# A list scheduler for the last step of the first MoE, and a unit's first group between the products of the unit before it

## The chip, the cores and the metric

The kernel runs on one core of a Trainium2 chip. Its engines are TensorE (PE, matrix products; PEld its weight loads), VectorE (DVE), ScalarE (ACT), GpSimd (POOL) and SyncE (SP, which here issues all the DMAs). Each executes its own instructions strictly in program order and waits on semaphores for the others. The metric is the device time of one execution in microseconds (us). The trace is of one execution, and times in it count from the span's start.

## The reference

Delta-rule attention over 4 batches, 8 heads, 768 positions gives 3072 tokens of 384 numbers. They go through a dense leaky feed-forward layer (the first MoE) and then through eight experts (the second MoE):

```python
h = x @ w_in                                  # 384 -> 2048
x2 = np.maximum(0.01 * h, h) @ w_out          # 2048 -> 384
P = exp(x2 @ w_gate - max)                    # 3072 x 8
for _ in range(8):                            # row and column sums in turn
    P /= P.sum(1, keepdims=True) + 1e-09
    P /= P.sum(0, keepdims=True) + 1e-09
    P *= N / E
out = sum(P[:, e:e+1] * (np.maximum(x2 @ w1[e], 0) @ w2[e]) for e in range(8))   # 384 -> 1024 -> 384
```

All in fp32; the kernel splits each operand into a high and a low part and multiplies three times (high by high, low by high, high by low).

## The kernel before

**Steps and chunks.** The tokens are cut into six steps of 512 (`TB`: 128 positions of each of 4 batches). In a step the first MoE (`main_a`, L647) runs over 16 chunks of 128 hidden units. A chunk's first product is nine matmuls 128x512 into a `ph` bank (L632); ACT scales it by 0.01 (`leak`, L669), DVE takes the maximum (L670), ACT rounds it to the high part `gh` (L672), DVE or POOL subtracts for the low part `gl` (L674); the second product is nine matmuls into three `po` banks (L684). PE computes chunk i's first product, then chunk i-1's second one.

**Step 5**, the last one, is special: no attention is left, and beside it the second MoE is prepared as a background (`pre_c`). Between two pieces of `main_a` it emits a little of it: the scales from the maxima (`powers`, L572 to L592); for five steps of tokens the load of x2 (`load_x`) into a staging tile `stg` (there are four), its parts `gxh` (ACT, L837) and `gxl` (DVE, L838) and six matmuls for the gate (L700); for four chunk pairs of the first expert's weights the load, a scaling (ACT, L841), four sums each for w1 and w2 (POOL, L868 and L887), the high parts (ACT, L873 and L892) and low parts (POOL, L874 and L893); and the operands `xoh`, `xol` of two token steps (L849 to L854). `Stage` keeps the loads ahead. Every engine's order is the order in which the program writes this down.

**The second MoE** is 24 units: 8 experts e by 3 pairs p of token steps. Its products are by Strassen and Winograd: seven products of sub-blocks in place of eight, with sums of operands and results around them. A unit has four `Group`s (first products: 33 matmuls 128x512 each, L1040, in f16, with some fifteen DVE and ACT operations that make the seven hidden operands h0..h6 with high and low parts), and four `Pair`s of seven second products (12 matmuls 128x192 each, L1133). After a product DVE adds the bank to the output sums with the gate's weight (`put`, written at the helper L1018, for the first expert L1015 or a copy at L1164). In the first expert's units the Sinkhorn rounds run beside the products.

All of that is written as operations of a `Plan` (L57): each has an engine, a modelled duration, what it reads and writes, and a due time; the plan starts on each engine the ready operation with the earliest due time, and emits all of them in the order of the planned starts. PE's due times follow the order in which its operations are written. The helpers make all instructions from a few lines: L1012 is every ACT copy, L1015 every two-operand subtraction or sum, L1018 every fused one, on DVE unless POOL is named.

**Banks and ends of units.** There are eight PSUM banks: `b0` to `b5` and two named `ph` (6 and 7). Pair i keeps products 1, 6, 7 in bank x, products 4, 5, 3 in bank 6 whatever the pair, product 2 in bank 2:

```python
self.x, self.y, self.z = (0, 1, 5, 7 if e else 0)[i], 6, 2
```

After eleven products of mixed pairs, a pair's last four come together (6, 5, 7, 3), pair after pair. Product n of a pair takes the hidden operand that `PRODUCTS` names: product 6 takes h4, 5 takes h3, 7 takes h5 and 3 takes h6. A bank that was started anew has to be read by its `put` before PE may start it again. Behind the last product the program writes a `clear` matmul (L1322) and then the next unit's four groups; the planner draws two products of them, into b5, in front of the old unit's last two.

Of the kernel before, what the change touches and what calls it, by code (L numbers as in the profile page):

```python
# [57 lines left out]
class Plan:  # L58
# [27 lines left out]
    def run(self):  # L86
# [17 lines left out]
        while len(done) < len(self.ops):  # L104
# [28 lines left out]
def delta_moe_kernel(ctx: ExitStack, tc: tile.TileContext, k_l, v_l, q_l, beta_l, wa_in, wg, wc, out):  # L133
# [8 lines left out]
    def fr(ap):  # L142
        return ap.bitcast(F32)
# [507 lines left out]
    def main_a(t):  # L651
# [5 lines left out]
        for i in range(n + 1):  # L657
            k = first + i
            if i < n:
# [14 lines left out]
                (dve if t in (0, 1, NT - 1) else pool).tensor_tensor(out=gl, in0=g, in1=fr(gh), op=ALU.subtract)  # L674
# [12 lines left out]
        for c in range(KD):  # L687
            o = g_p.tile([128, TB], F32, tag="gl" if c == 2 else "leak", name="x2o")
            act.activation(out=o, in_=po[c], func=ACTF.Copy)
            dve.tensor_reduce(out=xmax[:, t, c:c + 1], in_=po[c] if t == NT - 1 else o, axis=AX.X, op=ALU.max,  # L690
# [4 lines left out]

    def gate_block(xh, xl, t, ps_fn, lt, ordered=lambda ins: None):
        ps = ps_fn()
        for i, x in enumerate((xh, xl)):
            for c in range(KD):
                ordered(pe.matmul(out=ps[0:32], lhsT=wg_r[:, c], rhs=x[c] if isinstance(x, list) else x[:, c],  # L700
                                  start=(i == 0 and c == 0), stop=(i == 1 and c == KD - 1)))
            yield
        ordered(dve.transpose(out=lt.rearrange("p g e -> p (g e)"), in_=ps[0:32]))
        ordered(dve.tensor_tensor(out=logits[:, t * TB // 32:(t + 1) * TB // 32], in0=lt[:, :, 0:E],
                                  in1=lt[:, :, E:2 * E], op=ALU.add))
        yield

    if True:
# [119 lines left out]
        def staging():  # L828
            return cst_p.tile([128, KD * TB], F32, tag="stg", name="stg")

        def load_x(t):
            s = staging().rearrange("p (c n) -> p c n", c=KD)
            sp.dma_start(out=s, in_=x2_dram[t].rearrange("c p n -> p c n"))
            return s

        def parts(hi, lo, src, lo_eng):
            act.activation(out=hi, in_=src, func=ACTF.Copy)  # L837
            lo_eng.tensor_tensor(out=lo, in0=src, in1=fr(hi), op=ALU.subtract)  # L838

        def scaled(x, col):  # L840
            ordered(act.activation(out=x, in_=x, func=ACTF.Copy, scale=scl[:, col:col + 1]))  # L841

        def make_xo(s, t, tt):
            i, flat = t % 2, s.rearrange("p c (n k) -> p (c n) k", n=2)
            scaled(s, 2 * E + t)
            yield
            for o, x, y in ((tt[:, 0], flat[:, 1], flat[:, 0]), (tt[:, 1], flat[:, 3], tt[:, 0]),
                            (tt[:, 2], flat[:, 3], flat[:, 1]), (tt[:, 3], flat[:, 2], tt[:, 1])):
                pool.tensor_tensor(out=o, in0=x, in1=y, op=ALU.subtract)  # L849
            yield  # L850
            for j, src in ((slice(0, 1), flat[:, 0:1]), (slice(1, 5), flat[:, 2:6]), (slice(5, 9), tt)):
                hi, lo = (x[:, j, i] for x in xo)
                ordered(act.activation(out=hi, in_=src, func=ACTF.Copy))
                pool.tensor_tensor(out=lo, in0=src, in1=hi, op=ALU.subtract)  # L854
                yield

        def load_w1(n):
            e, k = divmod(n, NF2 // 2)
            s = staging()[:, 0:1280].rearrange("p (j f) -> p j f", f=128)
# [34 lines left out]

        def none(arg, s):
            pass

        W1, W2 = (load_w1, sums_w1, make_w1), (load_w2, sums_w2, make_w2)

        class Stage:  # L900
# [529 lines left out]
```

## Time and profile before

| | |
|---|---|
| median of three runs | 2382.3 us (2381.95 to 2382.96) |
| the profiled execution, its span | 2374.54 us, 2372.8 us |
| attention with steps 0 to 4 of the first MoE | 0 to 844 us |
| step 5 with the preparation | 844 to 947 us |
| second MoE, first expert | 947 to 1139 us |
| second MoE, experts 1 to 7 | 1139 to 2369 us |

A window row gives the stretch, its length, then the busy time, with the number of instructions, of PE, PEld, DVE, ACT and POOL in this order, then PE's granted clock (1.00 is 2.4 GHz, 0.50 is 1.2 GHz), the DMA engines' busy share and GB/s. Length less PE's busy time is PE's idle time. A timeline row gives start, duration, engine, line, output and inputs; in brackets stands how long the engine was idle just before, and what ended that.

### The profile page before, as it was taken

What the parts mean: (1) busy time and instruction counts of PE and PEld (TensorE: products, weight loads), DVE (VectorE), ACT (ScalarE), POOL (GpSimd) and SP (SyncE); (2) the same over time, 40 slices, a digit from 0 to 9 for tenths busy, and PEclk for the clock granted to TensorE, in tenths of its full rate; (3) what the DMA queues carried; (4) which work ended last, traced back from release to release, by engine and by line L of the source; (5) the groups of instructions that cost most, each with busy time, mean ns of one, the idle gap of its engine ahead of it and who ended that gap; (6) DMA issues with size and microseconds to landing.
All of it is one profiled execution on the core that took longest, in us unless ns stands there. A gap on an engine that the chain in (4) does not pass through costs nothing.

```text
span 2372.8 us, 43674 instructions
## 1 busy us (share of the span) xinstructions
PE 2200.5 (93%) x17324; PEld 1664.1 (70%) x17324; DVE 1702.5 (72%) x3304; ACT 1432.9 (60%) x2632; POOL 680.9 (29%) x748
## 2 busy tenths in 40 slices
PE   6788799999999988989999999999999999999999
PEld 5676677777777766666667677677677677677676
DVE  8567876848574254888677777777777777777777
ACT  6878757465655554666766655655655655656554
POOL 5444402132332254222411421321311312312100
PEclk7678999989999999999999999999999999999999
DMA  3354575545544353323323323323323333323221
GB/s 115 123 187 157 188 264 166 182 157 165 200 150 145 122 211 127 106 76 140 121 101 121 114 101 121 114 101 121 114 100 122 117 109 123 109 103 131 98 102 51
DMA packets 123453, 312.90 MB, mean 132 GB/s; under 512 B 14960, under 2 KB 66800, under 8 KB 117104
## 3 DMA queue, kind: packets, MB, share of 16 engines
q1 hardware_dynamic: 123248, 310.11, 38.2%
q8 instruction: 136, 2.23, 0.4%
q14 instruction: 69, 0.57, 0.1%
HBM read 247.84 MB, written 62.13 MB: 131 GB/s over the span
## 4 chain that ended last, share of the span: by engine, by line
PE 57%; DVE 8%; ACT 2%; POOL 2%; issue 1%; DMA 0%; SPq 0%; DVEq 0%; ACTq 0%; POOLq 0%
PE b L1040 18%; PE ph L1133 13%; PE ph L1040 10%; PE b L1133 10%; PE po L684 1%; PE ph L632 1%; DVE acc L1018 1%; DVE h26l L1015 1%; DVE h36l L1015 1%; DVE c L1018 1%; DVE h35l L1015 1%; DVE h16l L1015 1%; POOL stg L887 0%; DVE gxl L838 0%; POOL w1l L874 0%
## 5 line engine op out<-in xcount | busy, mean ns | idle before, releaser
L1015 POOL TENSOR_TENSOR stg<-stg 128x128 f32<-128x128 f32 (+2 forms) x240 | 157.4, 676 | 900.0 <-ACT stg L1012 896.0
L1040 PEld LDWEIGHTS <-w1h 128*128 128x128 f16 x2112 | 206.2, 98 | 241.6 <-issue 7.9
L1040 PE MATMUL b<-xoh,w1h 128*128 128x512 f16 x672 | 254.7, 379 | 0.0
L1040 PE MATMUL b<-xoh,w1l 128*128 128x512 f16 x672 | 254.7, 379 | 0.0
L1040 PE MATMUL b<-xol,w1h 128*128 128x512 f16 x672 | 254.7, 379 | 0.0
L684 PE MATMUL po<-gh,w 128*128 128x512 f32 (+1 forms) x600 | 221.2, 412 | 11.6 <-ACT gh L672 11.4
L1018 DVE SCALAR_TENSOR_TENSOR acc<-ph,pm,acc 128x192 f32<-128x192 f32 x315 | 134.8, 428 | 134.2 <-PE ph L1133 132.6
L1012 ACT ACTIVATE b<-ph 128x512 f32<-128x512 f32 x288 | 165.9, 584 | 72.6 <-PE ph L1040 66.7
L1040 PEld LDWEIGHTS <-w1l 128*128 128x128 f16 x1056 | 103.4, 98 | 124.6
L632 PE MATMUL ph<-x1h,w 128*128 128x512 f32 (+1 forms) x600 | 184.4, 414 | 4.9 <-DMA w<-wa_scratch 2.9
L1018 DVE SCALAR_TENSOR_TENSOR c<-b,v 128x512 f32<-128x512 f32 x96 | 66.1, 688 | 137.5 <-PE b L1040 131.6
L1012 ACT ACTIVATE v<-b 128x512 f32<-128x512 f32 x96 | 57.1, 595 | 173.6 <-PE b L1040 172.3
L670 DVE TENSOR_TENSOR leak<-leak,ph 128x512 f32<-128x512 f32 (+1 forms) x100 | 66.0, 660 | 117.6 <-ACT leak L669 115.0
L1040 PE MATMUL ph<-xoh,w1h 128*128 128x512 f16 x384 | 145.5, 379 | 4.2 <-ACT b L1012 4.2
L1040 PE MATMUL ph<-xoh,w1l 128*128 128x512 f16 x384 | 145.5, 379 | 0.0
L1040 PE MATMUL ph<-xol,w1h 128*128 128x512 f16 x384 | 145.5, 379 | 0.0
L684 PEld LDWEIGHTS po<-gh,w 128*128 128x128 f32 x600 | 117.3, 198 | 36.9 <-ACT gh L672 16.6
L1012 ACT ACTIVATE c<-b 128x512 f32<-128x512 f32 x192 | 114.3, 595 | 40.7 <-PE b L1040 39.9
L1015 DVE TENSOR_TENSOR c<-c,c 128x512 f32<-128x512 f32 x192 | 134.2, 705 | 1.4
L1018 DVE SCALAR_TENSOR_TENSOR c<-c,c 128x512 f32<-128x512 f32 x192 | 131.6, 698 | 2.0
L684 PE MATMUL po<-gl,w 128*128 128x512 f32 (+1 forms) x300 | 123.9, 414 | 9.5 <-POOL gl L674 6.0
L632 PEld LDWEIGHTS ph<-x1h,w 128*128 128x128 f32 x600 | 113.1, 201 | 27.3 <-DMA w<-wa_scratch 3.3
(433 smaller groups left out, 6924.1 us busy)
## 6 DMA issues: line engine op xcount, KB each, us to landing
w<-wa_scratch SPq DMA_DIRECT2D x100, 768.0 KB, 4.4
acc_scratch<-acc SPq DMA_DIRECT2D x84, 384.0 KB, 2.7
acc<-acc_scratch SPq DMA_DIRECT2D x84, 384.0 KB, 3.7
wraw<-wc SPq DMA_DIRECT2D x128, 192.0 KB, 3.3
stg<-wc SPq DMA_DIRECT2D x64, 384.0 KB, 8.7
xoh<-xo_scratch SPq DMA_DIRECT2D x21, 1152.0 KB, 5.1
xol<-xo_scratch SPq DMA_DIRECT2D x21, 1152.0 KB, 8.2
raw<-wa SPq DMA_DIRECT2D x48, 256.0 KB, 3.0
```

Source lines behind the costliest of these rows:

```text
L632: pe.matmul(out=ps, lhsT=wt[:, c * 128:(c + 1) * 128], rhs=xx[:, c], start=(n == 0), stop=(n == 3 * KD - 1))
L670: dve.tensor_tensor(out=g, in0=g, in1=ps, op=ALU.max)
L684: pe.matmul(out=po[c][:, cols], lhsT=wt[:, DM + c * 128:DM + (c + 1) * 128], rhs=xx, start=(i == 1 and m == 0), stop=(i == n and m == 2), ...
L1012: return vec("ACT", n, lambda e: e.activation(out=out, in_=src, func=func, scale=scale), reads, writes, **kw)
L1015: return vec(eng, n, lambda e: e.tensor_tensor(out=out, in0=a, in1=b, op=fn), reads, writes, **kw)
L1018: return vec("DVE", n, lambda e: e.scalar_tensor_tensor(out=out, in0=a, scalar=scalar, in1=b, op0=f0, op1=f1), reads, writes, **kw)
L1040: ordered(pe.matmul(out=banks[b], lhsT=w[:, a], rhs=x[:, c].rearrange("p s k -> p (s k)"), start=start, stop=i == 2 and (a, c) == terms[-1 ...
L1133: ordered(pe.matmul(out=banks[b][:, 0:HD], lhsT=xx[:, o:o + 128], rhs=wt[:, t], start=first and k == 0 and j == 0, stop=k == NK - 1 and j ...
```

## The change

Three edits:

1. In `Plan.run` a PE operation that follows another PE operation may be planned as soon as PE is free, not after the other's latency.
2. Step 5 of the first MoE and the preparation are written as operations of a plan of their own, with chunk i's second product behind two thirds of chunk i+1's first product as the written order. A gate's six matmuls become one piece. The sums of the first expert's weights go from POOL to DVE (`eng="DVE"`), and the parts of w2 are made in three pieces (192, 576, 576 columns) instead of two. The maxima at the step's end are taken from the copies, not from the `po` banks. `gate_block`, `Stage` and the loaders go.
3. In the second MoE banks are given out anew, the products of different pairs alternate to the end, and a group is cut into seven steps. The next unit's first group (`ahead`) runs its steps between the unit's last five products, except where the next unit's operands are still being made on the chip (two of the first expert's ends). The loads of the next operands are written behind the last group, not at the unit's end. For the first expert the copies after a product go from DVE to ACT.

```diff
@@ Plan.run
-                s.ready = max(s.ready, end + (self.WAIT if s.eng != e else 0.0))
+                s.ready = max(s.ready, end + self.WAIT if s.eng != e else free[e] if e == "PE" else end)
@@ step 5
-        bgq.add("pre_c", pre_c)
-        for _ in main_a(NT - 1):
-            bgq.spend(1.0, 2)
-        while bgq.pending():
-            bgq.pump(2)
+        tasks = {}
+        for n, t in enumerate((2, 3, 4, 0, 1)):
+            tasks[(2, 5, 8, 10, 12)[n]] = (n, t)
...
+        for i in range(NF1):
+            if i + 1 < NF1:
+                first_of(i + 1, (0,))
+            if i:
+                cks[i - 1].second()
+                if i + 3 < NF1:
+                    last = [cks[i + 3].load(last)]
+            if i in tasks:
+                n, t = tasks[i]
+                s, j = load_step(t)
+                gate(t, s, j, n)
+                if t < 2:
+                    operands(t, s, j)
+                else:
+                    weight1(t - 2, eng="DVE")
+                    weight2(t - 2, eng="DVE")
+            if i + 1 < NF1:
+                first_of(i + 1, (1, 2))
+        weight1(3, eng="DVE")
+        weight2(3, eng="DVE")
+        cks[NF1 - 1].second()
...
+        plan.run()
@@ Group: banks; head and body become seven steps with a yield behind each
-                self.x, self.y, self.z, self.w, self.v = 7 - k % 2 if e else 6, 2, 3, 4, 5
+                self.x, self.y, self.z, self.w, self.v = k % 2 * 7, 1, 3, 4, 5 if k else 3
@@ Pair: banks
-                self.x, self.y, self.z = (0, 1, 5, 7 if e else 0)[i], 6, 2
+                self.x, self.y, self.z = (0, 1, 5, 7)[i], 6 if e else 3 + i % 2, 2
+                self.y5 = (6, 2, 6, 2)[i] if e else (3, 4, 2, 2)[i]
@@ Pair.put
                 if self.e == 0 and fresh:
-                    vec("DVE", n, lambda e: e.tensor_copy(out=o, in_=src), [("ps", b)], [("acc", blk)])
+                    copy(n, o, src, [("ps", b)], [("acc", blk)])
@@ order of the products
-            for i, q in [(i, q) for i in range(4 if e else 3) for q in (6, 5, 7, 3)]:
+            for i, q in [(1, 1), (0, 2), (0, 4), (2, 1), (1, 2), (1, 4), (3, 1), (2, 2), (2, 4), (3, 2), (3, 4),
+                         (0, 6), (1, 6), (2, 6), (3, 6), (0, 5), (1, 5), (0, 7), (0, 3), (1, 7), (1, 3), (2, 5)]:
                 x[i].product(q)
                 if (i, q) == (0, 6):
                     mark = [x[0].last]
...
+            if nxt and not made:
+                ahead = Group(*nxt, 0)
+                it = ahead.steps()
+                clear(1, hb[0][S1][0][:, 0:128], hb[0][S1][0], [("h", 0, S1, 0)])
+                next(it)
+            for i, q in ((3, 5), (2, 7), (2, 3), (3, 7), (3, 3)) if e else ((2, 7), (2, 3), (3, 5), (3, 7), (3, 3)):
+                x[i].product(q)
+                if ahead:
+                    next(it)
...
+            for _ in it if ahead else ():
+                pass
```

**What moves on ACT in step 5.** These are ACT's rows before, near the end of the preparation (`w1h`, `w2h`: high parts of weights; `leak`, `gh`: a chunk of the first MoE; in brackets what a row waits for):

```order
L873 ACTIVATE w1h_9558<-stg 128x384
L669 ACTIVATE leak<-ph 128x512 [waits PE_49]
L873 ACTIVATE w1h_9558<-stg 128x768
L841 ACTIVATE stg<-stg,scl 128x768 [waits DMAHW2_49]
L672 ACTIVATE gh<-leak 128x512 [waits DVE_49]
L892 ACTIVATE w2h_9568<-stg 128x192 [waits Activation_49]
L892 ACTIVATE w2h_9568<-stg 128x1152 [waits Pool_49]
L669 ACTIVATE leak<-ph 128x512 [waits PE_49]
```

And these are the rows at the same place of the changed kernel, where L945 and L949 are the chunk's two operations and L835 is every copy of the preparation:

```order
L835 ACTIVATE stg<-stg,scl 128x768 [waits DMAHW0_49,Pool_49]
L835 ACTIVATE w2h_9566<-stg 128x576
L945 ACTIVATE leak<-ph 128x512 [waits PE_49]
L835 ACTIVATE w2h_9568<-stg 128x192 [waits Activation_49]
L949 ACTIVATE gh<-leak 128x512 [waits DVE_49]
L835 ACTIVATE w1h_9558<-stg 128x768 [waits DVE_49]
L835 ACTIVATE w2h_9568<-stg 128x576
L945 ACTIVATE leak<-ph 128x512 [waits PE_49]
L949 ACTIVATE gh<-leak 128x512 [waits DVE_49]
L835 ACTIVATE w2h_9568<-stg 128x576
```

Before, the copy 128x1152 that waits for POOL's sums stands ahead of a chunk's `leak`. After, no high part there waits for POOL (the scaling waits for its staging tile to be free), the large one is two pieces, and never more than two operations of the preparation stand between two of the chunks'.

**What moves on PE at the end of a unit.** PE's rows before (L1133 with h03h begins product 5 of a pair, with h05h product 7, with h06h product 3; L1322 is the clear; L1040 with b5 belongs to the next unit's first group, w1h0, and its second, w1h1; the rows left out are weight loads and the further matmuls of each product):

```order
L1133 MATMUL ph_10349<-w2h4_9570,h03h_10276 128x192 [waits DVE_49]
...
L1133 MATMUL ph_10350<-w2h4_9570,h05h_10280 128x192 [waits DVE_49]
...
L1133 MATMUL ph_10349<-w2h4_9570,h06h_10282 128x192 [waits DVE_49]
...
L1322 MATMUL b2_10345<-h00h_10270 128x512
...
L1040 MATMUL b5_10348<-xoh_9546,w1h0_9552 128x512 [waits DVE_49]
...
L1133 MATMUL ph_10349<-w2h4_9570,h03h_10276 128x192 [waits DVE_49]
...
L1040 MATMUL b5_10348<-xoh_9546,w1h1_9554 128x512 [waits Activation_49]
...
L1133 MATMUL ph_10349<-w2h4_9570,h06h_10282 128x192 [waits DVE_49]
...
L1040 MATMUL ph_10350<-xoh_9546,w1h0_9552 128x512 [waits DVE_49]
```

PE's rows of the changed kernel (L1182 is a second product, L1308 the clear, L1083 a first product; xoh with w1h0 belongs to the next unit):

```order
L1182 MATMUL ph_10342<-w2h2_9566,h03h_10269 128x192 [waits DVE_49]
...
L1308 MATMUL b1_10337<-h03h_10269 128x512 [waits DVE_49]
...
L1083 MATMUL b0_10336<-xoh_9546,w1h0_9552 128x512 [waits DMAHW3_49]
...
L1182 MATMUL b2_10338<-w2h2_9566,h03h_10269 128x192 [waits DVE_49]
...
L1083 MATMUL b3_10339<-xoh_9546,w1h0_9552 128x512
...
L1182 MATMUL b5_10341<-w2h2_9566,h05h_10273 128x192
...
L1083 MATMUL b0_10336<-xoh_9546,w1h0_9552 128x512 [waits Activation_49]
...
L1182 MATMUL ph_10342<-w2h2_9566,h06h_10275 128x192 [waits DVE_49]
...
L1083 MATMUL b1_10337<-xoh_9546,w1h0_9552 128x512
...
L1182 MATMUL ph_10343<-w2h2_9566,h05h_10273 128x192
...
L1083 MATMUL b0_10336<-xoh_9546,w1h0_9552 128x512 [waits Activation_49]
```

Before, the last products alternate between the two `ph` banks, most of them wait for DVE's `put` of an earlier one, and two first products stand among them. After, each of the last five products has a step of the next group's seven in front of it, and the five go to four banks.

## Rows read from the trace of the kernel before

**Rows 1.** Windows of three stretches: step 5, first expert, the other seven.

```profile
844.10:947.20 103.10, 84.11 (x322) 60.71 (x321) 54.10 (x76) 53.38 (x84) 60.73 (x62) 0.92 0.49 175
947.20:1138.60 191.40, 179.16 (x1438) 126.58 (x1438) 155.61 (x319) 116.27 (x192) 57.60 (x61) 0.99 0.31 110
1138.60:2369.40 1230.80, 1195.81 (x9851) 860.57 (x9848) 944.20 (x1680) 732.57 (x1294) 283.71 (x331) 0.99 0.31 109
```

**Rows 2.** Waits of PE in step 5: total us, times, longest.

```profile
PE po L684 <- ACT gh L672: 6.3, 4, 2.3
PE gate L700 <- ACT gxh L837: 4.0, 2, 3.0
PE po L684 <- DVE gl L674: 3.4, 3, 2.0
PE gate L700 <- DVE gxl L838: 2.6, 4, 1.3
```

**Rows 3.** Chain of waits, end of step 5: start, us, what.

```profile
930.75 2.04 PE ph L632 x9
...
945.28 1.90 DVE xmax L690 x3
```

**Rows 4.** Groups of step 5: busy us, mean ns; idle before and its releasers.

```profile
L887 POOL TENSOR_TENSOR stg<-stg 128x192 f32<-128x192 f32 x16 | 11.4, 733 | 0.2
...
L868 POOL TENSOR_TENSOR stg<-stg 128x128 f32<-128x128 f32 x16 | 10.3, 666 | 16.4 <-ACT stg L841 16.1
...
L838 DVE TENSOR_TENSOR gxl<-stg,gxh 128x512 fp32r<-128x512 f32 x15 | 16.1, 1106 | 5.6 <-ACT gxh L837 3.4 <-DMA stg<-wc 2.2
L674 DVE TENSOR_TENSOR gl<-leak,gh 128x512 fp32r<-128x512 f32 x16 | 15.3, 957 | 14.2 <-ACT gh L672 14.2
```

**Rows 5.** Timeline of DVE and POOL at 860 us.

```profile
860.85 2.45 DVE L674 TENSOR_TENSOR gl<-leak,gh 128x512 fp32r<-128x512 f32 x1 [3.79 <-ACT gh L672]
...
860.38 2.37 POOL L893 TENSOR_TENSOR w2l<-stg,w2h 128x1152 f16<-128x1152 f32 x1 [1.27 <-ACT w2h L892]
```

**Rows 6.** Windows within step 5.

```profile
844.10:850.00 5.90, 5.14 (x24) 3.67 (x23) 5.05 (x13) 3.76 (x8) 0.00 (x0) 1.00 1.00 355
860.00:870.00 10.00, 7.14 (x18) 4.48 (x19) 7.58 (x8) 7.42 (x14) 7.63 (x8) 0.66 0.44 159
```

**Rows 7.** Waits of PE, first expert.

```profile
PE ph L1133 <- DVE acc L1164: 6.7, 4, 2.4
PE ph L1040 <- ACT b L1012: 4.2, 6, 1.0
```

**Rows 8.** Waits of PE, experts 1 to 7.

```profile
PE ph L1133 <- DVE acc L1018: 17.6, 21, 1.0
PE b L1133 <- DVE acc L1018: 17.4, 8, 2.8
```

**Rows 9.** Windows of two units of expert 5, clear to clear.

```profile
1841.27:1901.46 60.19, 56.77 (x472) 40.77 (x470) 46.53 (x80) 38.17 (x67) 24.17 (x27) 1.00 0.33 117
1901.46:1958.96 57.50, 56.60 (x471) 40.76 (x470) 44.58 (x80) 31.30 (x56) 6.94 (x7) 1.00 0.27 99
```

**Rows 10.** Timeline of PE and DVE near those units' ends.

```profile
1890.42 0.24 PE L1133 MATMUL b<-w2h,h05h 128*128 128x192 f16 x1 [2.44 <-DVE acc L1018]
...
1892.55 0.24 PE L1133 MATMUL ph<-w2h,h06h 128*128 128x192 f16 x1 [0.98 <-DVE acc L1018]
...
1950.06 0.24 PE L1133 MATMUL ph<-w2h,h06h 128*128 128x192 f16 x1 [0.90 <-DVE acc L1018]
...
1889.36 0.68 DVE L1015 TENSOR_TENSOR h35l<-c,h35h 128x512 f16<-128x512 f32 x1
1889.96 0.41 DVE L1018 SCALAR_TENSOR_TENSOR acc<-b,pm,acc 128x192 f32<-128x192 f32 x1
```

**Rows 11.** Windows of 20 us, units of expert 3: groups, products.

```profile
1440.00:1460.00 20.00, 20.00 (x95) 9.10 (x93) 18.88 (x31) 17.73 (x34) 0.00 (x0) 1.00 0.06 21
1480.00:1500.00 20.00, 20.00 (x173) 14.79 (x172) 8.35 (x18) 11.06 (x20) 15.26 (x23) 1.00 0.53 170
```

More of the change, by code (lines that the diff above doesn't have):

```diff
@@ L843, in make_xo @@
[L843 to L855, printed above, removed]
@@ new lines, in gate, with emit @@
+        def gate(t, s, j, g):
+            for c in range(KD):
+                copy(TB, gx[0][:, c], s[:, c], [("stg", j)], [("gx", 0, c)])
+                tensor(TB, gx[1][:, c], s[:, c], fr(gx[0][:, c]), ALU.subtract, [("stg", j), ("gx", 0, c)],
+                       [("gx", 1, c)], shared=True)
+            b, P = gb[g % 2], ("bg", g % 2)
+            def emit():
+                for i in range(2):
+                    for c in range(KD):
+                        ordered(pe.matmul(out=b[0:32], lhsT=wg_r[:, c], rhs=gx[i][:, c], start=i == 0 and c == 0,
+                                          stop=i == 1 and c == KD - 1))
+            op("PE", 2 * KD * MR, 2 * KD * MR + 0.15, emit, [("gx", i, c) for i in range(2) for c in range(KD)], [P])
+            op("DVE", 0.7, 0.8, lambda: [ordered(dve.transpose(out=lt.rearrange("p g e -> p (g e)"), in_=b[0:32]))],
+               [P], ["lt"])
+            op("DVE", 0.3, 0.4, lambda: [ordered(dve.tensor_tensor(
+                out=logits[:, t * TB // 32:(t + 1) * TB // 32], in0=lt[:, :, 0:E], in1=lt[:, :, E:2 * E],
+                op=ALU.add))], ["lt"], [("logits", t)])
@@ new lines, in delta_moe_kernel @@
+        for i in range(2, 4):
+            last = [cks[i].load(last)]
+        gen = powers(0, NSC, lambda name: gb[2], ordered)
+        first_of(0, (0,))
+        for eng, us in (("PE", 0.4), ("DVE", 1.0), ("PE", 0.4), ("DVE", 1.4)):
+            op(eng, us, us + 0.1, lambda: next(gen), [("bg", 2)], [("bg", 2)])
+        first_of(0, (1, 2))
+        for i in range(NF1):
[16 more added lines that the diff above has]
+                first_of(i + 1, (1, 2))
@@ L1025, in delta_moe_kernel @@
+        rate = 170e3
         class Group:
@@ L1332, in delta_moe_kernel @@
                     dma(128 * 9 * TB * 2, xo_dram[p, i], xo[i].rearrange("p j s k -> p (j s k)"), XO, [("xod", p, i)])
-            gs = [Group(e, p, k) for k in range(NK)]
+            gs = [ahead] if ahead else [Group(e, p, 0)]
+            gs += [Group(e, p, k) for k in range(1, NK)]
             for k, g in enumerate(gs):
-                g.head()
+                if not ahead or k:
+                    it = g.steps()
+                    next(it)
                 if k:
                     gs[k - 1].tail()
-                g.body()
+                for _ in it:
+                    pass
             if e:
@@ L1341, in delta_moe_kernel @@
                 load(e, p, 2)
+            nxt = units[u + 1] if u + 1 < len(units) else None
+            made = e == 0 and p < 2
             x = [Pair(e, p, i) for i in range(4)]
@@ L1354, in delta_moe_kernel @@
                     mark = [x[0].last]
-            if not e:
-                for q in (1, 2, 4, 6, 5, 7, 3):
-                    x[3].product(q)
-            if u + 1 < len(units):
-                clear(2, hb[0][A11][0][:, 0:128], hb[0][A11][0], [("h", 0, A11, 0)])
-            n = (e + 1) * NK
-            if e == 0 and p < 2:
+            n = (e + 1) * NK
+            ahead = None
+            if e == 0:
+                for b in (3, 4):
+                    clear(b, hb[0][S1][0][:, 0:128], hb[0][S1][0], [("h", 0, S1, 0)])
+            if nxt and not made:
+                ahead = Group(*nxt, 0)
[5 more added lines that the diff above has]
+                if ahead:
+                    next(it)
+            if nxt and made:
+                clear(1, hb[0][S1][0][:, 0:128], hb[0][S1][0], [("h", 0, S1, 0)])
                 ss = [load_step(t) for t in (2 * p + 2, 2 * p + 3)]
```

384 lines of the change are left out of this document (171 added, 213 removed).

## Prediction

> **What bounds the kernel now.** First the table of windows: in all three stretches that the change touches PE is the busiest engine, but not to the same degree. Its idle time is the length less its busy time: step 5 has 103.10 - 84.11 = 19.0 us, the first expert 191.40 - 179.16 = 12.2 us, experts 1 to 7 1230.80 - 1195.81 = 35.0 us [rows 1]. Step 5 is also the one with a low clock, 0.92. Second, PE's waits, stretch by stretch, to see who ends the idle time: in step 5 four different lines of ACT and DVE [rows 2], in the second MoE almost only DVE's additions to the output [rows 7, 8]. Third, what those engines did then: the groups and timelines [rows 4, 5, 10]. So PE's own work is the floor, and the change is worth what it takes away of 66 us of idle time and of the time at half clock.
>
> **Step 5, the floor.** 16 chunks of 2 x 9 matmuls are 288, and 30 are for the gates. After the preparation has ended, a chunk's nine take 2.04 us without a gap [rows 3], so 0.227 each: 288 x 0.227 = 65.3 and 30 x 0.227 = 6.8, together 72.1 us. Around it stand the start and the end. At the end PE's first clear waits for three maxima that DVE reads from the very banks to be cleared, 1.90 us behind a first copy [rows 3]; the changed kernel takes the maxima from ACT's copies, so the bank is free after the copies; I put 1.2 us for the end, and 0.9 us for the scales' transpose, which stands early in the new order. A step 5 without any other wait is 72.1 + 2.1 = 74 us, 29 less than the 103.1 of now.
>
> **Step 5, the waits that stay.** They are 6.3 + 4.0 + 3.4 + 2.6 = 16.3 us [rows 2], and what the low clock adds behind them (0.66 on the mean from 860 to 870 us, of levels that are 1.00 and 0.50 [rows 6]). Their cause is the program order: ACT takes copies of weights that wait for POOL's sums while a chunk's `leak` or `gh` is queued behind, and a gate's matmuls stand on PE ahead of a chunk that is ready. POOL's sums are 11.4 + 10.3 = 21.7 us of its 60.7 [rows 1, 4]. The changed order puts one chunk operation after every two operations or so of the preparation, waits for all parts of a gate before its six matmuls, and moves the 21.7 us to DVE. DVE has 54.1 us of 103.1 busy now [rows 1]. Nearest to the new operations on DVE are POOL's own rows, 0.67 to 0.73 us each [rows 4], of 128 or 192 columns, and DVE's `gl` of 512 columns, at 0.96 on the mean with its delays [rows 4]. By the one the 32 sums would cost DVE 22 us; by their share of `gl`'s width (0.25 and 0.375), 16 x 0.24 + 16 x 0.36 = 10 us, which is my estimate, since the engine and the operation are the same. DVE is then at 64 of about 80 us, ACT at its 53, POOL at 60.7 - 21.7 = 39. That is tighter than now, on an engine whose order mixes sums that wait for a load with the `gl` that PE waits for. The bounds are a gain of 29 (no wait stays) and of 0 (all stay, as the wait for DVE replaces the one for POOL). I take 20, nearer to the floor, since the stretch after the preparation shows PE at full rate with these same chunk operations on ACT and DVE [rows 3], and the waits that go are those that POOL's sums set. Each of the queues has cover: the DMAs move 175 GB/s x 103 us = 18 MB in the step, which at the 355 GB/s of its first 6 us [rows 1, 6] is 51 us.
>
> DVE and POOL do hinder each other here: `gl` took 2.45 us at 860.85 where POOL's `w2l` ran from 860.38 for 2.37 us [rows 5]. The Trainium skill, SBUF — State Buffer, section Who interferes with whom, has the rule: DVE and GpSimd share one pair of SBUF ports under an exclusive lock. The trace agrees with the rule by the 2.45 us. By it POOL holds DVE for less of the time, 39 instead of 61 us, but DVE has 32 more instructions to be held; were every second sum held for 1 us, DVE would be at 80 of 80 us and the gain of step 5 near half of the one I take.
>
> **Experts 1 to 7.** Here I go from clear to clear. A regular unit takes 57.50 us with PE busy 56.60; the first unit of expert 5, 60.19 [rows 9]. With 14 regular units in 1230.80 us the other seven take (1230.80 - 14 x 57.50) / 7 = 60.8 each. If a unit were PE's 56.6 and nothing else, 14 x 0.9 + 7 x 4.2 = 42 us would go; 35.0 of that is idle time [rows 1], the rest is the clock. What sets the waits is the banks: product 3 of a pair waits until DVE has read the bank of product 5, 0.90 us at 1950.06 and 21 such waits in all, 17.6 us; in the longer units product 7 waits besides, 2.44 us at 1890.42, for a `put` that stands on DVE behind the low part h35l, which ended at 1890.04 [rows 8, 10]. In the longer units the wait is thus for DVE's whole chain, which has fallen behind, and a free bank alone would not help.
>
> Yet DVE is not short of time over the unit: 44.6 to 46.5 us of 57 to 60 [rows 9]. It is short in the groups (18.9 of 20 us) and idle in the products (8.4 of 20) [rows 11]. The change gives it work earlier: the next unit's first group starts on PE some five products, 5 us, before the unit's end, so its subtractions fall into the idle stretch. By the same token the first group's 33 matmuls no longer run at the unit's start with nothing else for PE to do. Product 5 of three pairs and both 7 and 3 are put further from what they wait for by one to three products of about 1 us (2.13 us between two starts less the 0.98 of idle time, at 1892.55 [rows 10]). I count 2 us for the earlier group and 2 us for the later products, 4 us of slack against 0.9 in a regular unit and 3.4 (2.44 + 0.98, [rows 10]) in a longer one. So the regular units lose all of their 0.9, 12.6 us, and the longer ones, where the slack just covers the wait, 3.2 of 4.2, 22.4 us. The sum is 35 us. Bounds: 42, and from below 0 or less, if the interleaved group makes waits of its own: its second step needs ACT's copy of the first, and the clear waits for a `put`. These are covered by a product of 1 us each, against ACT operations of 17.7 / 34 = 0.5 us on the mean [rows 11]. The extra clears, six in the kernel, are matmuls like the others, 1 to 2 us in all.
>
> **First expert.** Its waits are 6.7 us for DVE's copies and 4.2 for ACT [rows 7]. The copies go to ACT, busy 116 of 191 us where DVE has 156 [rows 1], and the pairs get banks apart. I take 7 of the 12 us. Bounds: 12, and 0: the next units' operands come from POOL, which has 16 products after its mark instead of 19, so a wait of 1 to 2 us at two boundaries may come.
>
> **Sum.** 20 + 35 + 7 = 62 us off the profiled execution's 2374.5 gives 2312.5. The median of the runs lies 7.8 us above that execution, so 2320.
>
> **Rivals.**
> *DVE or the loads bound step 5.* DVE's `gl` and `gxl` mean 0.96 and 1.11 us where a subtraction of that width takes 0.68 in the second MoE [rows 4, 10]; in the new order 32 sums that each wait for a load and a scaling stand among them, and one late load holds a chunk. If 10 us of that come on PE's path, the gain is 10 instead of 20: 2330. For it: staging has four tiles as before, and `gxl` already waited 2.2 us for a load [rows 4]. Against: DVE would still be under its time.
> *The waits at the ends of units only move.* The planner's durations are not the chip's; if DVE's chain stays late by 2 to 3 us in the longer units and the regular ones get a wait of 0.5 for ACT's copy or the clear, experts 1 to 7 give 12 rather than 35: 2343. For it: at 1890 the wait was for the chain, not the bank [rows 10]. Against: DVE's idle share in the products [rows 11].
> *The interleaved group makes the ends worse.* Place: the five product-and-step pairs. PE takes instructions in order; if steps wait for ACT and products for DVE by turns, twice a wait like the 2.44 [rows 10] at each of 22 ends, 22 x 4.9 = 107 us come on top of the forecast: 2427. It makes the kernel slower from (62 + 4.8) / 22 = 3.0 us of new waits an end. Against: on no row does ACT hold PE for long in experts 1 to 7 [rows 8].
> *It does little.* Step 5 stays bound by its preparation and the ends keep their waits, so only the maxima at its end (2 us), some banks and the copies (8 us) show: 2372.
>
> **Chances.** Forecast 0.64 (its own range 2304 to 2330), DVE or loads in step 5 0.15, ends only move 0.11, little 0.05, worse 0.05. A measurement of this kernel tells from no change about 0.2%, 4.8 us. Slower is the worse case, 0.05; within 0.2% falls 0.03 of the case that it does little; the rest, 0.92, is faster. The range 2300 to 2348 goes from all three upper bounds (29 + 42 + 12 = 83 us off, 2299) to beyond the second rival.
>
> **What would show it.** Step 5: clears at about 927 instead of 947; PE busy 76 of 83 us; no wait for `gxh`; a wait for `gl` at most of 1 us, and POOL down by 20 us. If PE's list names DVE with more than 10 us there, the first rival holds. Experts 1 to 7: units of 56.7 (regular) and 57.5 to 58 (the first of an expert), waits for DVE's `put` under 10 us in all. If the first units still take 60, or a wait for ACT's copy shows at each end, the second or third does. The forecast is wrong as a whole if the time is over 2348.

## The result, and the profile after

The changed kernel takes 2308.5 us (median of four runs, 2300.7 to 2312.9) against 2382.1 (four runs, 2376.5 to 2383.0): a ratio of 0.9702, 95% interval 0.9672 to 0.9731. Forecast were 2320 us in a range of 2300 to 2348. The medians differ by 73.6 us. The profiled execution took 2312.9 us, 4.4 above its median, while the one of before lay 7.6 below its own.

The three stretches in windows of the changed kernel's trace (columns as in [rows 1]):

```profile
853.20:939.90 86.70, 77.97 (x322) 57.38 (x321) 66.06 (x105) 52.94 (x88) 42.06 (x34) 0.98 0.60 217
939.90:1131.30 191.40, 189.54 (x1502) 131.37 (x1502) 149.86 (x283) 139.84 (x262) 66.13 (x69) 1.00 0.35 125
1131.30:2307.70 1176.40, 1173.14 (x9792) 849.61 (x9789) 948.91 (x1673) 723.06 (x1275) 276.95 (x324) 1.00 0.32 112
```

PE's idle time, length less busy time, is 8.7 us in step 5 where it was 19.0 [rows 1], 1.9 near the first expert, 3.3 in the rest where it was 35.0. In step 5 PE's busy time fell as well, from 84.1 to 78.0 us for the same 322 matmuls, with the granted clock up from 0.92 to 0.98: of the gain there 10.3 us are idle time and 6.1 busy time. The last two windows do not begin and end with a unit now, since the next unit starts inside the old one; so I compare the second MoE as a whole, from the start of the first of its clears to the start of its last matmul: 1422.1 us before, 1367.5 after.

| stretch | before | after | difference | forecast |
|---|---|---|---|---|
| up to step 5 (same code) | 844.0 | 853.2 | +9.2 | 0 |
| step 5, its first product to the first clear | 103.2 | 86.7 | -16.5 | -20 |
| second MoE | 1422.1 | 1367.5 | -54.7 | -42 |

The first line of the table is not the change: in the 14 traces of this study step 5 begins between 839.1 and 856.9 us, with the same code ahead of it. All that follows is therefore read from stretches, not from whole times.

PE's waits in step 5, in the first expert and in the others (engine, line, who ended the wait, us in total, times, longest):

```profile
PE po L958 <- ACT gh L949: 4.4, 5, 1.8
PE po L958 <- DVE gl L950: 2.6, 2, 1.6
PE gb L572 <- DVE cmax L693: 1.0, 1, 1.0
PE b L1308 <- ACT x2o L1031: 0.8, 1, 0.8
...
PE b L1182 <- DVE acc L838: 1.0, 1, 1.0
...
PE b L1182 <- ACT acc L835: 0.6, 1, 0.6
...
PE b L1182 <- DVE acc L841: 1.9, 2, 1.1
PE ph L1182 <- DVE acc L841: 1.4, 2, 1.0
```

The waits for the gate's parts are gone (6.6 us in [rows 2]), the 10.9 us for the first expert [rows 7] are 1.6, and the 35.0 for DVE's additions [rows 8] are 3.3, all of it in the first unit of expert 1. The units of expert 5, from clear to clear, which were 60.19 and 57.50 [rows 9]:

```profile
1794.71:1851.78 57.07, 57.07 (x474) 41.05 (x473) 46.39 (x80) 39.12 (x69) 22.96 (x27) 1.00 0.35 121
1851.78:1907.56 55.78, 55.78 (x469) 40.46 (x467) 45.09 (x80) 31.83 (x57) 11.54 (x13) 1.00 0.31 107
1907.56:1963.98 56.42, 56.42 (x471) 40.73 (x470) 45.21 (x80) 34.00 (x59) 9.37 (x12) 1.00 0.35 124
```

PE is busy for the whole of each. They differ because the clear now stands before a unit's last products; the mean is 56.42, PE's own work. At the end of the first of them, on PE (a first product of the next unit, then products 7 and 3 of pair 0) and on DVE (the low parts that these two need):

```profile
1846.18 0.38 PE L1083 MATMUL b<-xoh,w1h 128*128 128x512 f16 x1
...
1846.83 0.25 PE L1182 MATMUL b<-w2h,h05h 128*128 128x192 f16 x1
...
1847.82 0.25 PE L1182 MATMUL ph<-w2h,h06h 128*128 128x192 f16 x1
...
1844.59 0.68 DVE L838 TENSOR_TENSOR h35l<-c,h35h 128x512 f16<-128x512 f32 x1
...
1846.72 0.68 DVE L838 TENSOR_TENSOR h36l<-c,h36h 128x512 f16<-128x512 f32 x1
1847.32 0.41 DVE L841 SCALAR_TENSOR_TENSOR acc<-ph,pm,acc 128x192 f32<-128x192 f32 x1
```

Product 3 starts at 1847.82. Its last operand, h36l, ended at 1847.40. The last row is the `put` of product 5, which frees the bank (6, for products 5 and 3 of pair 0 in both kernels); it ended at 1847.73. Where PE waited for this `put`, it started 0.05 us after it (1950.01 and 1950.06, rows below), so the first units make it by some 0.04 us, where DVE was behind at 1890 [rows 10]. And a product of the next unit's first group, three matmuls and 0.65 us, has slipped in front of the two, by the planner's choice and not by the written order.

Step 5's operations on DVE (busy us, mean ns), against [rows 4]; L838 with stg on DVE are the sums that were POOL's:

```profile
L838 DVE TENSOR_TENSOR stg<-stg 128x192 f32<-128x192 f32 (+1 forms) x32 | 21.1, 688 | 2.1 <-ACT stg L835 1.9
...
L838 DVE TENSOR_TENSOR gxl<-stg,gxh 128x512 fp32r<-128x512 f32 x15 | 14.1, 977 | 1.6 <-ACT gxh L835 1.6
...
L950 DVE TENSOR_TENSOR gl<-leak,gh 128x512 fp32r<-128x512 f32 x16 | 12.7, 791 | 3.7 <-ACT gh L949 3.6
```

The sums take 21.1 us, as much as on POOL (21.7), not the 10 of the forecast. Half of the 32 are 128x192, half 128x128. The timeline shows why:

```profile
906.92 2.25 DVE L838 TENSOR_TENSOR stg<-stg 128x192 f32<-128x192 f32 x1
...
914.38 0.34 DVE L838 TENSOR_TENSOR stg<-stg 128x192 f32<-128x192 f32 x1
...
906.35 2.60 POOL L838 TENSOR_TENSOR xol<-stg,xoh 128x1024 f16<-128x1024 f32 x1
```

The same sum of 128x192 takes 0.34 us with POOL idle and 2.25 us when it meets POOL's low part, which runs to 908.95; the sum ends at 909.17, 0.2 us later.

### The profile page after: what moved, and what is told of

The parts are those of the page before. It is cut to its first block, busy times and chain, and to the rows that moved or that the text cites. A ratio compares the mean times of both kernels' runs of the same rounds, so it can differ in the third digit from the quotient of the medians.

```text
span 2310.9 us, 43775 instructions
## 1 busy us (share of the span) xinstructions
PE 2191.4 (95%) x17330; PEld 1665.7 (72%) x17330; DVE 1715.8 (74%) x3288; ACT 1447.0 (63%) x2684; POOL 664.0 (29%) x720
## 4 chain that ended last, share of the span: by engine, by line
PE 76%; ACT 10%; DVE 8%; issue 3%; DMA 2%; POOL 2%; SPq 0%; ACTq 0%; DVEq 0%; POOLq 0%
PE b L1083 24%; PE b L1182 18%; PE ph L1182 10%; PE ph L1083 5%; PE ph L632 4%; PE po L684 3%; PE y_ps L437 2%; PE w_ps L428 2%; ACT a_d L296 2%; ACT x L362 2%; DMA wraw<-wc 1%; ACT p L378 1%; ACT u L388 1%; PE g_ps L280 1%; PE m_ps L347 1%
## 5 line engine op out<-in xcount | busy, mean ns | idle before, releaser
L838 POOL TENSOR_TENSOR stg<-stg 128x128 f32<-128x128 f32 (+2 forms) x248 | 165.9, 687 | 813.9 <-ACT stg L835 809.6
L1083 PEld LDWEIGHTS <-w1h 128*128 128x128 f16 x2112 | 204.9, 98 | 220.7 <-issue 1.4
L1083 PE MATMUL b<-xoh,w1h 128*128 128x512 f16 x864 | 327.5, 379 | 0.0
L1083 PE MATMUL b<-xoh,w1l 128*128 128x512 f16 x864 | 327.5, 379 | 0.0
L1083 PE MATMUL b<-xol,w1h 128*128 128x512 f16 x864 | 327.5, 379 | 0.0
L841 DVE SCALAR_TENSOR_TENSOR acc<-b,pm,acc 128x192 f32<-128x192 f32 (+1 forms) x357 | 155.3, 448 | 92.5 <-PE b L1182 91.6
L1083 PEld LDWEIGHTS <-w1l 128*128 128x128 f16 x1056 | 103.3, 98 | 124.7
L684 PE MATMUL po<-gh,w 128*128 128x512 f32 (+1 forms) x504 | 185.2, 411 | 4.9 <-ACT gh L672 4.8
L835 ACT ACTIVATE b<-b 128x512 f32<-128x512 f32 x144 | 84.1, 584 | 140.4 <-PE b L1083 138.7
L841 DVE SCALAR_TENSOR_TENSOR acc<-ph,pm,acc 128x192 f32<-128x192 f32 (+1 forms) x231 | 97.9, 432 | 77.0 <-PE ph L1182 76.9
L835 ACT ACTIVATE c<-b 128x512 f32<-128x512 f32 x192 | 113.9, 593 | 62.9 <-PE b L1083 61.9
L838 DVE TENSOR_TENSOR c<-c,c 128x512 f32<-128x512 f32 x192 | 136.0, 712 | 2.5
L838 POOL TENSOR_TENSOR w2l<-stg,w2h 128x576 f16<-128x576 f32 (+1 forms) x96 | 109.4, 1160 | 73.7 <-ACT w2h L835 73.7
L670 DVE TENSOR_TENSOR leak<-leak,ph 128x512 f32<-128x512 f32 (+1 forms) x84 | 55.1, 656 | 91.7 <-ACT leak L669 86.7
L674 POOL TENSOR_TENSOR gl<-leak,gh 128x512 fp32r<-128x512 f32 x48 | 62.2, 1295 | 188.8 <-ACT gh L672 176.4
L838 POOL TENSOR_TENSOR w1l<-stg,w1h 128x384 f16<-128x384 f32 (+1 forms) x64 | 85.4, 1340 | 34.9 <-ACT w1h L835 34.9
```

Of the source, the lines that this page charges most:

```text
L670: dve.tensor_tensor(out=g, in0=g, in1=ps, op=ALU.max)
L674: (dve if t in (0, 1) else pool).tensor_tensor(out=gl, in0=g, in1=fr(gh), op=ALU.subtract)
L684: pe.matmul(out=po[c][:, cols], lhsT=wt[:, DM + c * 128:DM + (c + 1) * 128], rhs=xx, start=(i == 1 and m == 0), stop=(i == n and m == 2), ...
L835: return vec("ACT", n, lambda e: e.activation(out=out, in_=src, func=func, scale=scale), reads, writes, **kw)
L838: return vec(eng, n, lambda e: e.tensor_tensor(out=out, in0=a, in1=b, op=fn), reads, writes, **kw)
L841: return vec("DVE", n, lambda e: e.scalar_tensor_tensor(out=out, in0=a, scalar=scalar, in1=b, op0=f0, op1=f1), reads, writes, **kw)
```

## The experiments

In each the stretches are read from the trace: step 5 (86.7 us in the changed kernel, 103.2 before) and the second MoE (1367.5 and 1422.1). A unit's length is from clear to clear.

**Each half by itself.** Step 5 as changed, the second MoE as before:

```diff
-                ahead = Group(*nxt, 0)
-                it = ahead.steps()
+            gs = [Group(e, p, k) for k in range(NK)]
...
+                self.x, self.y, self.z, self.w, self.v = 7 - k % 2 if e else 6, 2, 3, 4, 5
+                self.x, self.y, self.z = (0, 1, 5, 7 if e else 0)[i], 6, 2
+                self.y5 = self.y
```

> The changed kernel with the second MoE as before (banks, order of the products, no group ahead, the first expert's copies on DVE, the old rule of the planner there): step 5 alone is changed. Read from the trace: step 5 from its first product to the first clear (103.2 us before, 86.7 after the change), the second MoE from that clear to the last product (1422.2 before, 1367.5 after). Theory, the two parts are independent: step 5 86 to 88, second MoE 1419 to 1425, the whole 16 us (0.7%) under before. Rival, step 5 ends so tight that it hands late operands to the second MoE: step 5 as after, but the second MoE 1427 or more, and the gain under 11 us.

Measured: step 5 87.1, second MoE 1423.5, ratio to before 0.9934 (0.9909 to 0.9960). PE's waits from there on are those of before, 18.0 and 15.8 us for DVE's additions in experts 1 to 7 ([rows 8]: 17.6 and 17.4). The halves are independent.

**Without the group ahead.**

```diff
-            if nxt and not made:
-                ahead = Group(*nxt, 0)
...
-                next(it)
+            if nxt:
+                clear(1, hb[0][S1][0][:, 0:128], hb[0][S1][0], [("h", 0, S1, 0)])
```

> The changed kernel without the group ahead: the five last products of a unit come without steps of the next group between them; banks, order of the products and early loads stay. Theory, the early start of the next group gives DVE its chain earlier and so takes the waits at the ends away: the second MoE gets back some 20 us of its 55 (1380 to 1400), the first units of an expert 59 us or more, with PE waiting for DVE's additions again. Rival, the new banks and the alternating order do it: 1372 or less, units of 56.4 to 56.7 each, no such waits.

Measured: step 5 86.7, second MoE 1382.4. First units take 59.3 us, the two others of an expert 55.78 and 56.86 (a mean of 56.3). PE's waits in experts 1 to 7 of this kernel:

```profile
PE ph L1182 <- DVE acc L841: 7.2, 8, 1.0
PE b L1182 <- DVE acc L841: 3.9, 8, 0.8
PE ph L1083 <- ACT b L835: 3.2, 12, 0.3
```

The time lies in the theory's range, the units in between. The group ahead is worth 15 of the 54.7 us, nearly all in the first units. The 0.9 us of the regular units stays away without it, so the other edits of the second MoE do that. The next four runs look for which.

**The old written order of the last products**, new banks, no group ahead:

```diff
-                         (0, 6), (1, 6), (2, 6), (3, 6), (0, 5), (1, 5), (0, 7), (0, 3), (1, 7), (1, 3), (2, 5)]:
+                         ] + ([(i, q) for i in range(3) for q in (6, 5, 7, 3)][:11] if e else
...
```

> As without the group ahead (second MoE 1382.4 us, first units of an expert 59.3), and for experts 1 to 7 the old written order of the last products (a pair's 6, 5, 7, 3 together, pair after pair) with the new banks. Theory, the banks carry that part of the gain, since with two banks for products 5 and 3 the planner alternates the pairs by itself: second MoE 1379 to 1388. Rival, the written order carries it: 1395 or more, with waits of 0.9 in each unit again.

**And with one bank for products 4, 5 and 3:**

```diff
-                self.y5 = (6, 2, 6, 2)[i] if e else (3, 4, 2, 2)[i]
+                self.y5 = 6 if e else (3, 4, 2, 2)[i]
```

> As the one with the old written order and without the group ahead, and with one bank (6) for products 4, 5 and 3 of all pairs again in experts 1 to 7. Theory, the banks carry it: the waits of product 3 for the put of product 5 come back, 0.9 in each unit and more in an expert's first, second MoE 1400 to 1412 (20 to 28 us over the one with two banks). Rival, the banks matter little, and the rest of the change there (the early loads, the clear, the banks of the groups) does it: 1390 or less.

Measured: 1393.9 and 1381.3. The first is near the rival's bound, yet not by the waits it named: its regular units take 56.4, and only the first ones got longer, to 59.4 to 61.2 from expert 2 on. The second falls on the rival's side: one bank is enough. There the planner by itself put products of the next unit's first group (three matmuls each) between the old unit's last ones, five at the end of expert 5's first unit and one at the end of its second; from expert 3 on first units take 58.0, regular ones 56.4 to 56.8.

**The old banks for the groups and the clear**, no group ahead:

```diff
-                self.x, self.y, self.z, self.w, self.v = k % 2 * 7, 1, 3, 4, 5 if k else 3
+                self.x, self.y, self.z, self.w, self.v = (7 - k % 2, 2, 3, 4, 5) if e else (k % 2 * 7, 1, 3, 4, 5 if k else 3)
```

> The changed kernel without the group ahead, and with the groups of experts 1 to 7 on the banks of before (x in 6 and 7, y in 2), which the last products of the pairs use too. Theory, the waits of 0.9 us in the regular units before came from a late start of the next unit's groups, which found their banks still held by the last products: regular units 57.2 to 57.6 again against 56.4, second MoE 1395 to 1412 (1382.4 with the new banks). Rival, the order of the products or the early loads did it: regular units 56.4, second MoE 1386 or less.

Measured: 1384.7, regular units 56.4, first units 58.8 to 60.5. My theory fell a second time. I then took the place of product 3 of pair 0 in PE's order for the cause, the first product to need h36l. The last of these runs puts all of the settings back at once:

> Experts 1 to 7 with the groups' banks, the bank of products 4, 5 and 3, the clear's bank and the written order of before and without the group ahead, in one kernel; the early loads, the planner's rule and the changed first expert stay. PE's order is then that of before: 17 second products stand in front of the first product 3, which needs DVE's last low part h36l, with nothing from the next unit among them (19 in the changed kernel, 17 and three wide matmuls in the two with only one of the old settings). Theory, that place is what made the 0.9 of the regular units: they take 57.2 to 57.6 again, first units 60 to 61.5, second MoE 1402 to 1412. Rival, the early loads, the rule or the first expert did it: regular units 56.4, second MoE 1386 to 1396.

Measured: 1408.5, most regular units 57.5, first units 58.1 to 61.9. PE's waits in experts 1 to 7 of this kernel:

```profile
PE ph L1182 <- DVE acc L841: 18.0, 21, 1.0
PE b L1182 <- DVE acc L841: 16.2, 8, 2.8
```

That is [rows 8] again, 21 and 8 waits, so these settings together carry the waits. But the place in the order is not the whole cause. The 0.9 (0.83 to 0.90) is in 11 of the 14 regular units of the kernel before. The other three, the last of expert 1 and the last two of expert 7, have 17 products ahead as well and no wait; they are the three in which POOL, which prepares the next expert's weights, did not delay the low parts that DVE makes for product 3. Rows of the kernel before, in the second unit of expert 5 and then in the second of expert 7, with the window of the latter:

```profile
1945.54 3.59 POOL L1015 TENSOR_TENSOR stg<-stg 128x192 f32<-128x192 f32 x4 [44.42 <-ACT stg L1012]
...
1948.60 1.07 DVE L1015 TENSOR_TENSOR h36l<-c,h36h 128x512 f16<-128x512 f32 x1
1949.60 0.41 DVE L1018 SCALAR_TENSOR_TENSOR acc<-ph,pm,acc 128x192 f32<-128x192 f32 x1
...
2299.46 0.68 DVE L1015 TENSOR_TENSOR h36l<-c,h36h 128x512 f16<-128x512 f32 x1
...
2300.76 0.25 PE L1133 MATMUL ph<-w2h,h06h 128*128 128x192 f16 x1
...
2253.22:2309.67 56.45, 56.45 (x473) 40.75 (x470) 43.35 (x80) 28.73 (x52) 0.00 (x0) 1.00 0.28 95
```

The same read from the timelines, in us from the first second product of a unit; the delay is what the six low parts of h5 and h6 take in all over 0.68 us each:

| regular unit | products ahead of product 3 | PE gets there | h36l ends | delay of low parts | wait |
|---|---|---|---|---|---|
| before, and all settings old | 17 | 17.0 | 17.5 | 1.3 | 0.9 |
| before, expert 7, POOL idle | 17 | 16.8 | 16.2 | 0.0 | 0 |
| old order | 17 and three wide matmuls | 17.5 | 16.0 | 0.0 | 0 |
| old order, one bank | 16 | 15.8 | 15.4 | 0.7 | 0 |
| no group ahead, new or old banks for the groups | 19 | 18.8 | 18.4 | 1.6 | 0 |
| changed kernel | 19 | 18.8 | 16.4 | 0.8 | 0 |

(All but the second row are the second unit of expert 5.) With the old order and one bank only 16 products stand ahead, and there is no wait, so distance alone does not explain it. What decides is whether DVE's chain is done when PE arrives. In the kernel before, POOL's operations made the chain 1.3 us late, more than the wait; two products more ahead cover even 1.6 us, and with the old order alone POOL starts only after h36l.

So of the 54.7 us some 41 (1408.5 to 1367.5) are for the banks, the order and the group ahead in experts 1 to 7. The other 13.6 belong to what that run kept: the changed first expert, the early loads and the planner's rule. A run below prices the rule at nothing there; the early loads were not tested by themselves.

**The first expert's copies on DVE again.**

```diff
-                    copy(n, o, src, [("ps", b)], [("acc", blk)])
+                    vec("DVE", n, lambda e: e.tensor_copy(out=o, in_=src), [("ps", b)], [("acc", blk)])
```

> The changed kernel with the first expert's copies after a product on DVE again. Theory, the move to ACT takes DVE's part of the first expert's waits away (6.7 us before): second MoE 1370 to 1375 against 1367.5, and PE waiting for DVE's copies before 1135 us. Rival, the banks kept apart do it: 1367 to 1369.

Measured: 1379.7, more than expected. At the end of the second unit PE waits twice for long for DVE's copies (L1213):

```profile
1050.59 0.32 PE L1182 MATMUL b<-w2h,h05h 128*128 128x192 f16 x1 [5.15 <-DVE acc L1213]
...
1056.08 0.32 PE L1182 MATMUL b<-w2h,h06h 128*128 128x192 f16 x1 [3.41 <-DVE acc L1213]
```

Without the move to ACT 12.3 of the 13.6 us are lost. The two waits are longer than any for a copy in the kernel before (2.4 [rows 7]), so the first expert's new order depends on the move, and the two can't be priced apart.

**The sums on POOL again.**

```diff
-                    weight1(t - 2, eng="DVE")
-                    weight2(t - 2, eng="DVE")
+                    weight1(t - 2)
+                    weight2(t - 2)
```

> The changed kernel with the sums of the first expert's weights back on POOL. Theory A, POOL's sums were what held ACT's copies and so the chunks: step 5 93 to 98 us against 86.7, POOL 62 us busy there, PE waiting for gh. Theory B, the order did it (a chunk's operations between the preparation's), and the engine of the sums hardly matters: 85 to 89. Theory C, DVE's 21 us of sums cost more than they bring, since POOL holds them up: under 85.

Measured: step 5 87.0, second MoE 1367.4: theory B. POOL is at 61.6 us, DVE at 52.3 instead of 66.1. In this kernel `gl` got slower, 1.18 us on the mean against 0.79:

```profile
L950 DVE TENSOR_TENSOR gl<-leak,gh 128x512 fp32r<-128x512 f32 x16 | 18.9, 1178 | 9.8 <-ACT gh L949 9.5
...
L838 POOL TENSOR_TENSOR stg<-stg 128x192 f32<-128x192 f32 (+2 forms) x40 | 27.1, 696 | 29.9 <-ACT stg L835 29.3
```

(the second row holds 8 sums of x as well). Moving the sums between the two engines left the length of step 5 as it was; the delay lands on another operation.

**The low parts of the weights on DVE as well**, POOL left with x:

```diff
-                tensor(m, lo[:, d], s[:, i], hi[:, d], ..., "POOL")
+                tensor(m, lo[:, d], s[:, i], hi[:, d], ..., eng)
```

> The changed kernel with the low parts of the first expert's weights on DVE as well, so that POOL has only the sums and low parts of the two token steps in step 5. Theory, the 32 sums take DVE 21.1 us (0.69 each) because POOL's operations hold them: they fall to 0.4 each or less, so that DVE stays at 62 to 70 us busy though it has 20 more operations, and step 5 takes 84 to 88 us (86.7). Rival, the sums are as slow by themselves: DVE at 76 us or more, and step 5 at 91 or more.

Measured: step 5 86.1, second MoE 1367.5; DVE 65.1 us busy with 125 operations where it had 66.1 with 105. In this kernel's step 5:

```profile
L838 DVE TENSOR_TENSOR stg<-stg 128x192 f32<-128x192 f32 (+1 forms) x32 | 11.9, 404 | 0.3
...
L838 DVE TENSOR_TENSOR w2l<-stg,w2h 128x576 f16<-128x576 f32 (+1 forms) x12 | 7.3, 611 | 0.0
```

The sums fall from 0.69 to 0.40 us on the mean, with POOL busy for 17.3 us instead of 42.1: POOL's operations had cost them 9 us. Its time is 2302.7 us in two runs, ratio to before 0.9685 (0.9647 to 0.9723), which is not told from the changed kernel.

**The sums planned as shared.**

```diff
+                tensor(HD, s[:, o], s[:, x], s[:, y], fn, r, [("sum", j, o)], eng, shared=eng == "DVE")
```

> The changed kernel with the sums on DVE planned as shared operations (the planner adds up to 0.8 us to one that meets POOL at work, as it does for gl and gxl). Theory, part of step 5's waits for gl and gh comes from a plan that takes the sums for short: 82 to 86 us against 86.7. Rival, the order hardly changes, or the preparation's end moves back: 86 to 90.

Measured: step 5 85.5, the shortest seen; second MoE 1367.5; 2305.9 us, ratio 0.9699 (0.9607 to 0.9790). The eight traces with the changed kernel's step 5 lie between 86.3 and 87.1 us, so this is a gain of about one, in one trace, and half a us inside the theory's range.

**The preparation earlier.**

```diff
-            tasks[(2, 5, 8, 10, 12)[n]] = (n, t)
+            tasks[(1, 3, 6, 8, 10)[n]] = (n, t)
```

> The changed kernel with the five tasks of the preparation written earlier in step 5 (behind chunks 1, 3, 6, 8, 10 instead of 2, 5, 8, 10, 12). Theory, step 5 is held by the end of the preparation, which is crammed into the last 20 us (PE busy 6.6 of 10 us from 920 to 930): 80 to 84 us against 86.7. Rival, the loads bound its start (the DMA share is 1.0 until 870), and earlier loads make the chunks' weights late: 87 or more, with PE waiting for a DMA.

Measured: step 5 91.4, the rival's time but not its cause. PE's waits in this kernel's step 5:

```profile
PE po L958 <- ACT gh L949: 5.2, 7, 1.4
PE po L958 <- DVE gl L950: 2.1, 3, 1.4
PE gb L973 <- DVE gxl L838: 2.1, 3, 1.3
...
PE ph L932 <- DMA w<-wa_scratch: 0.9, 1, 0.9
```

The weights came late only once (0.9 us); the largest sum is again `gh`, and the gate's matmuls wait for `gxl` as in the kernel before.

**The planner's old rule.**

```diff
-                s.ready = max(s.ready, end + self.WAIT if s.eng != e else free[e] if e == "PE" else end)
+                s.ready = max(s.ready, end + (self.WAIT if s.eng != e else 0.0))
```

> The changed kernel with the planner's old rule (an operation on PE behind another one on PE is planned after that one's latency). The written order of PE holds most of it, so I expect step 5 within 1.5 us of 86.7 and the second MoE within 4 us of 1367.5. Rival, the rule carries part of the gain, since the planner puts products in front of steps whose PE predecessor it thinks unfinished: second MoE 1375 or more.

Measured: step 5 87.9, second MoE 1367.4. Against 86.3 to 87.1 in the traces of the same step 5, the first of the three edits is worth about a us at most there, by one trace, and nothing in the second MoE.

## Why the prediction was right, and where its steps were off

The time lies in the forecast's own range. The sum took 62 us off, and the two profiled executions differ by 61.7. That they agree so closely is chance: the stretches that the change touches gave 71.2 us, and the part in front of them took 9.2 more in the one execution. So the sum was 9 us short, too high for step 5 and too low for the two others.

**Step 5: 20 forecast, 16.5 measured.** The size holds, the reason only in part. I had counted on two things: that the waits set by POOL's sums go because the sums leave POOL, and that chunk operations stand between those of the preparation. With the sums back on POOL the step takes the same 87.0 us, so it is not the engine of the sums. What is left is the rewritten step as a whole (its order, a gate in one piece, the pieces of w2, the maxima); these were not told apart, so that it is the order stays an argument. The term that was mis-sized is the 32 sums on DVE, 10 us: 21.1. The estimate by width, 0.36 for 192 columns, was right for an idle POOL (0.34 at 914.38), and POOL's operations cost the rest, as the 11.9 us of the run that takes the weights off POOL shows. The first rival (DVE or the loads bound the step) had 10 us on PE's path; the gain fell short by 3.5, and waits for DVE's `gl` are 2.6. The floor of 74 was too low: at a granted clock of 1.00, in the kernel with the low parts on DVE, PE was busy for 76.0 us, not 72.1. What holds the step at 85.5 to 87.9 us in every kernel but one is open: in the changed kernel PE's waits are 8.8 of it, half of them for `gh`, and the engine of the sums, the low parts, the planner's rule and its idea of a sum's length each moved it by little.

**Experts 1 to 7: 35 forecast, 41 measured.** The step that failed is the sentence that the banks set the wait of the regular units. In the unit of 1950.06, h36l ended at 1949.67 and the `put` that frees the bank at 1950.01. Since product 3 needs h36l too, a bank free at once would have brought it forward by some 0.3 of the 0.9 us, an estimate from these two rows. DVE's chain, 1.3 us late beside POOL, sets the rest; POOL is in no term of this part of the sum, and the wait was in 11 regular units, not in 14. That the longer units wait for the whole chain held. My count of slack there, 2 us for the group ahead and 2 for the later products against 3.4, came out close: the margin is 0.04 us. The size was off in these units too: I took 3.2 of their 4.2 us, and all of it went. Only a part of that is the clock. A unit of 60.2 had a granted clock of 1.00 [rows 9], so the clock is at most the 0.6 us from there to the mean of 60.8, 4 us over the seven. In the kernel with everything old, the first units of experts 3 and 4 are 60.2 and 61.7 us long with the same two waits of 2.44 and 0.98; the stretches around and behind the second wait read:

```profile
1515.00:1524.00 9.00, 8.36 (x102) 8.36 (x102) 5.65 (x14) 2.10 (x3) 8.92 (x12) 1.00 0.31 98
1690.00:1700.00 10.00, 9.17 (x94) 8.93 (x94) 5.42 (x14) 2.10 (x3) 9.27 (x12) 0.83 0.23 83
```

The first, at a granted clock of 1.00, belongs to the unit of 60.2, the second, at 0.83, to the one of 61.7.

**First expert: 7 forecast, 13.6 measured.** With the copies on DVE again 12.3 of it are lost. It is more than the upper bound of 12: some 4 us of it lie in the first unit of expert 1, which took 62.2 us before and 58.1 with everything else old. The wait of 1 to 2 us for POOL's operands at two boundaries did not come: no wait for POOL is in PE's list.

**The rivals.** That the waits only move: none did; the ends have neither a wait for ACT's copy nor one for the clear's `put`. That the ends get worse: 3.0 us of new waits an end would have been needed, and there are 0.

## What to carry to other kernels

Before a bank is blamed for a wait, look whether the waiting product has another input that the same engine finishes just before; then a free bank gives back only the difference. Look also for a round of the loop that has the same order and no wait: here it named GpSimd, whose work made VectorE's chain late. Such a wait goes when the chain ends earlier, or when independent work, as the next round's first products, stands in front of the waiting product. And work moved between VectorE and GpSimd takes their mutual delay with it, so price it beside the other's load, not alone.

## What the runs showed of the hardware

A DVE sum of two SBUF operands, 128x192, beside a running POOL operation ended just after it: 0.34 us alone, 2.25 us at 906.92 beside one that ended at 908.95. The 32 sums of step 5 took 21.1 us with POOL at 42 us of 86.7, and 11.9 with POOL at 17. In the second MoE of the kernel before, h36l took 0.68 us with POOL idle (2299.46) and 1.07 beside POOL (1948.60). The Trainium skill, SBUF — State Buffer, section Who interferes with whom, says that these two engines take turns on one shared pair of ports under an exclusive lock; the trace agrees. Also unexpected: the 840 us in front of the change, with the same code, differ by 17.8 us between executions (839.1 to 856.9), more than any experiment on step 5 moved; why is open.
